# Placing the norm steps of the next batch by when GpSimd has their input, in an attention and feed-forward kernel

## The chip, the cores and the metric

The kernel runs on one core of one Trainium2 chip. The metric is device time in microseconds (us). (The clock is the share of full speed that was granted to PE.)

Names of the engines as the profile has them: PE is TensorE, PEld its weight loads, DVE is VectorE, ACT is ScalarE, POOL is GpSimd, SP is the engine whose queue issues most DMAs. ACT and DVE take their instructions in program order.

## The reference, cut to what matters

```python
batch, n_heads, seq, head_dim = 8, 12, 448, 64
q_n, k_n = rmsnorm(q, g_q), rmsnorm(k, g_k)       # x / sqrt(mean(x*x) + 1e-6) * g
attn = softmax(q_n @ k_n.T / 8)
x = (attn @ v).transpose(0, 2, 1, 3).reshape(3584, 768)
h = x @ w_in                                       # 768 -> 2048
g = h + sin(alpha * h) ** 2 / alpha                # "snake"
out = g @ w_out                                    # 2048 -> 768
```

## The kernel before: the parts that matter

For each batch there is an attention stage (21 scores tiles `S`, each a set of small matmuls and one exp on ACT; 6 `A`, each the product with v and a normalization) and a first product (96 matmuls, with the snake on ACT, POOL and DVE). The second product of the *previous* batch is cut into 56 fillers `F` (two matmuls each) and laid between the S and A of the attention stage, so that PE has work while ACT does the exps. The numbers in `S_(3)` are warm-ups: matmuls on a blank tile, whose results nobody uses. Matmuls write to PSUM, a memory in banks; DVE copies (`osb`) take the second product out of it, and PE waits when no bank is free.

q and k come in three chunks per batch (`NC = 3`). Each chunk is normalized in steps, on three engines (1/sqrt is made of a Ln and an Exp):

```python
st.steps = (lambda: square(0), lambda: square(1), # 0, 1: POOL, q and k
            fold_g,                               # 2: POOL, q *= g_q*g_k
            lambda: reduce(0), lambda: reduce(1), # 3, 4: DVE, sums of the squares
            lambda: (rsqrt(), scale(0), scale(1)),# 5: ACT Ln and Exp, then POOL
            transpose)                            # 6: SP, DMA transposes
```

During the attention stage of batch b, the last steps of its own third chunk (c2) and nearly all steps of the next batch's first two (c3 and c4) are handed out over 24 slots of the plan:

```python
PLAN = "6 SS 7 SS 7 SSS 8 SSS 8 SSAS 7 SS 5 SSASA 4 S 4 SSAAA"   # numbers: fillers
at[s0].append(step_of(ci, 5))                 # c2, s0 = 2
at[s0 + 2].append(step_of(ci, 6))
if b + 1 < B:
    for ci in (NC * b + 3, NC * b + 4):       # c3 from slot 2, c4 from slot 10
        at[s0] += [lambda ci=ci: begin_norm(ci), step_of(ci, 0, 1, 2)]
        for n, step in ((4, 3), (5, 4), (6, 5), (8, 6)):
            at[s0 + n].append(step_of(ci, step))
        s0 += 8
```

`begin_norm(ci)` also loads chunk ci+2 into one of three buffers. A stage's place on the clock is written "+x" below: x us after the stage began.

## Time and profile before

| | before |
|---|---|
| time, median | 467.0 us |
| first product of batch 0 starts | 47.2 us |
| from there to the first product of batch 1 | 58.0 us |
| from one first product to the next, batches 1 to 6 | 53.44 us each |
| the same, batch 6 to 7 (no next batch to norm) | 50.35 us |
| from the last first product to the end | 43.4 us |

The starts of the eight first products are read from the chain of work that ended last; they mark the batches, because each is 18.28 us of matmuls without a stop. Sum of the stretches: 47.2 + 58.0 + 5 x 53.44 + 50.35 + 43.4 = 466.1, the profiled span. The lines themselves are in the prediction. Two more, from the list of who waited for whom over the whole span (us in total, times, longest):

```profile
ACT inv L235 <- DVE ms L226: 28.2, 13, 3.2
DVE ms L226 <- POOL sq L220: 21.6, 11, 5.6
```

ACT stood 28 us at the Ln of a norm and DVE 22 us at a reduce, each for want of its input.

### The profile page before, as it was taken

To read this page: it belongs to the slowest core of one execution; us is meant where nothing else is said; L and a number is where in the kernel's file an instruction comes from. 1 tells how busy PE (TensorE), PEld (TensorE's weight loads), DVE (VectorE), ACT (ScalarE), POOL (GpSimd) and SP (SyncE) were. 2 spreads that over 40 slices of the span, in tenths; PEclk is the share of its full clock that TensorE was granted. 3 is DMA by queue.
4 is the path that set the end of the run, shared out by engine and by line. 5 is a ranking of instruction groups with operands and counts; after the bars stand their busy time and mean duration, and the time that the engine had idled before them with its cause. 6 is when DMAs were issued, how large, how long until landed. Compare 5 with 4: busy or idle time off the path is not lost.

```text
span 466.1 us, 9452 instructions
## 1 busy us (share of the span) xinstructions
PE 431.0 (92%) x3810; PEld 224.4 (48%) x3812; DVE 227.7 (49%) x331; ACT 340.3 (73%) x531; POOL 278.1 (60%) x262
## 2 busy tenths in 40 slices
PE   7777996899998999989998999989998999999996
PEld 3235543455544555445544555445544555555563
DVE  3575572335734564445643546254644456144521
ACT  4768784587867788688877878767877878788800
POOL 3858869554699086963789266981879455201400
PEclk9788997999999999999999999999999999999999
DMA  6999997684065900787046920679026720410023
GB/s 237 192 242 241 232 170 211 148 108 114 0 147 161 203 28 2 189 178 168 1 111 184 166 76 1 163 178 195 3 77 151 89 63 1 108 36 18 1 50 86
DMA packets 69296, 55.09 MB, mean 118 GB/s; under 512 B 41460, under 2 KB 65796, under 8 KB 69252
## 3 DMA queue, kind: packets, MB, share of 16 engines
q1 hardware_dynamic: 56690, 40.97, 35.5%
q0 software_dynamic: 11616, 11.81, 17.8%
q10 hardware_dynamic: 946, 1.70, 1.0%
q8 instruction: 30, 0.49, 0.4%
q14 instruction: 14, 0.11, 0.1%
HBM read 45.62 MB, written 11.01 MB: 122 GB/s over the span
## 4 chain that ended last, share of the span: by engine, by line
PE 62%; ACT 11%; POOL 10%; DVE 9%; issue 5%; DMA 2%; SPq 0%; POOLq 0%; DVEq 0%
PE hps L343 31%; PE ops L388 14%; PE av L307 12%; ACT expT L294 7%; DVE ms L226 5%; POOL qkn L245 4%; POOL sq L220 4%; PE sc L291 4%; DVE xT L316 1%; ACT inv L235 1%; POOL s L325 1%; DVE g_sb L330 1%; PE sc L287 1%; DMA qkT<-qkn 1%; ACT inv L236 1%
## 5 line engine op out<-in xcount | busy, mean ns | idle before, releaser
L294 ACT ACTIVATE expT<-sc 128x896 bf16<-128x896 f32 x168 | 144.1, 912 | 30.8 <-PE sc L291 30.6
L388 PE MATMUL ops<-w_out_sb,g_sb 128*128 128x384 bf16 x896 | 159.9, 330 | 5.3 <-ACT expT L294 5.3
L343 PE MATMUL hps<-xT,w_in_sb 128*128 128x448 bf16 x768 | 146.7, 353 | 0.0
L325 POOL TENSOR_TENSOR s<-s 128x448 f32<-128x448 f32 x64 | 59.3, 930 | 120.0 <-ACT s L322 109.1
L388 PEld LDWEIGHTS <-g_sb 128*128 128x128 bf16 x896 | 83.5, 98 | 77.9 <-issue 27.4
L330 DVE SCALAR_TENSOR_TENSOR g_sb<-s,inv_alpha_sb,hps 128x448 bf16<-128x448 f32 x128 | 80.7, 677 | 63.1 <-POOL s L325 63.1
L343 PEld LDWEIGHTS <-w_in_sb 128*128 128x128 bf16 x768 | 74.3, 98 | 71.7 <-issue 2.9
L316 DVE TENSOR_TENSOR xT<-av,rec 64x448 bf16<-64x448 f32 x96 | 59.7, 622 | 88.8 <-ACT rec L311 69.7
L322 ACT ACTIVATE s<-hps,alpha_sb 128x448 f32<-128x448 f32 x128 | 74.5, 627 | 28.6 <-PE hps L343 26.7
L245 POOL TENSOR_TENSOR qkn<-qk,inv 128x448 bf16<-128x448 f32 x84 | 76.1, 937 | 28.1 <-ACT inv L236 21.3
L220 POOL TENSOR_TENSOR sq<-qk 128x896 f32<-128x896 f32 x42 | 69.9, 1678 | 7.4 <-DVE ms L226 5.6
L307 PE MATMUL av<-expT,vb 64*64 64x448 bf16 x672 | 70.7, 356 | 3.6 <-ACT expT L294 3.6
L307 PE MATMUL av<-expT,ones 64*64 64x448 bf16 x672 | 70.9, 356 | 0.0
L291 PE MATMUL sc<-qkT 64*64 64x448 bf16 x672 | 53.8, 374 | 15.0 <-ACT expT L294 7.5
L226 DVE TENSOR_REDUCE ms<-sq 128x14 f32<-128x896 f32 x42 | 44.9, 1082 | 21.9 <-POOL sq L220 21.6
L223 POOL TENSOR_TENSOR qk<-qk,gg 128x896 f32<-128x896 f32 x24 | 50.0, 2084 | 5.0 <-ACT gg L171 3.4
L394 DVE COPY osb<-ops 128x768 f32<-128x768 f32 (+1 forms) x35 | 27.9, 798 | 47.1 <-PE ops L388 46.3
L307 PEld LDWEIGHTS <-vb 64*64 64x64 bf16 x672 | 39.5, 109 | 15.9 <-issue 5.4
L307 PEld LDWEIGHTS <-ones 64*64 64x64 bf16 x672 | 38.6, 109 | 10.6
L327 ACT ACTIVATE s<-s 128x448 f32<-128x448 f32 x64 | 36.9, 577 | 2.8
L291 PEld LDWEIGHTS <-qkT 64*64 64x64 bf16 x672 | 16.4, 107 | 45.1 <-issue 40.4
L310 ACT ACTIVATE rec<-av 128x448 f32<-128x448 f32 x48 | 26.2, 545 | 4.1 <-PE av L307 3.6
(43 smaller groups left out, 137.6 us busy)
## 6 DMA issues: line engine op xcount, KB each, us to landing
qk<-in_q_dram SPq DMA_DIRECT2D x24, 448.0 KB, 6.1
qk<-in_k_dram SPq DMA_DIRECT2D x22, 448.0 KB, 6.9
out_dram<-osb SPq DMA_DIRECT2D x39, 192.0 KB, 4.6
vb<-in_v_dram POOLq DMA_DIRECT2D x32, 168.0 KB, 7.4
w_in_sb<-in_moe_w_in_dram POOLq DMA_DIRECT2D x2, 1536.0 KB, 19.3
w_out_sb<-in_moe_w_out_dram POOLq DMA_DIRECT2D x2, 1536.0 KB, 25.8
out_dram<-osb SPq DMA_DIRECT2D x26, 96.0 KB, 3.1
qk<-in_k_dram ACTq DMA_DIRECT2D x2, 448.0 KB, 5.8
```

The costliest lines, as they stand in the source:

```text
L220: nc.gpsimd.tensor_mul(st.sq[w], qk[ci][:, w], qk[ci][:, w])
L226: nc.vector.reduce_sum(st.ms[:, w, :], st.sq[w], axis=AX.X)
L245: eng.tensor_mul(n[:, :, hi, :], x[:, hi], inv[:, hi].unsqueeze(2).to_broadcast([P, NJ, D]))
L291: nc.tensor.matmul(sc[key_rows(pp, hi), pp, :S], qkt[r, 1, j * REST:(j + 1) * REST], qkt[r, 0, :], start=True, stop=True)
L294: nc.scalar.activation(expT[c, j], sc[:, :, :S], ACT.Exp, scale=SCALE)
L307: nc.tensor.matmul(av[o, part, :S], ones[r, :] if part else vb[b][r, hp, j, :], expT[pi // 2, j][r, pi % 2, :], start=(j == 0), stop=(j == ...
L316: nc.vector.tensor_mul(xT[b][r, hp, :], av[r, 0, :S], rec[o, :])
L322: nc.scalar.activation(s1, hps, ACT.Sin, scale=alpha_sb[:, m, :])
L325: nc.gpsimd.tensor_mul(s2, s1, s1)
L330: nc.vector.scalar_tensor_tensor(g_sb[:, m, (b % 2) * S:(b % 2 + 1) * S], s2, inv_alpha_sb[:, m, :], hps, op0=ALU.mult, op1=ALU.add)
L343: nc.tensor.matmul(ps[:, m % 2, :S], w_in_sb[:, kt, m * P:(m + 1) * P], x[:, kt, :], start=(kt == 0), stop=(kt == KT - 1))
L388: nc.tensor.matmul(st["ps"][:, k, :HALF], lhsT, w_out_sb[:, m, half * HALF:(half + 1) * HALF], start=(m == 0), stop=(m == MT - 1))
```

## The change

Its intent: give each norm step a slot by which its input exists, so that no in-order engine waits with ready work behind it. To fill POOL's wait for c3's Ln, the squares of c4 go ahead of c3's scale. The chunk loads move behind the transposes of the chunk that frees the buffer, and the loads of v go out two slots later. The order of batch 0, which has no second product to fill with, is redone by hand.

```diff
-                    lambda: (rsqrt(), scale(0), scale(1)), transpose)
+                    lambda: (rsqrt(), scale(0), scale(1)),
+                    lambda: (transpose(), load_qk(ci + 3) if ci + 3 < NC * B else None))
...
     def begin_norm(ci):
         norm[ci] = norm_tasks(ci)
-        if ci + 2 < NC * B and ci != NC + 2:
-            load_qk(ci + 2)
... (batch 0: S, A and warm-up matmuls in another order; its core:)
-    S_(), S_(3), S_(4)
+    S_(2), S_(1), S_()
     c1.pe_transpose((0, 1))
+    load_qk(NC + 1)
     c2.reduce(0), c2.reduce(1)
-    S_(), S_(3), A_(), S_()
+    S_(), S_(1), S_(1)
     c2.rsqrt()
     c2.scale(0), c2.scale(1)
...
-    S_(3), S_()
+    A_(), S_(1), S_(1), S_(1)
     c2.pe_transpose((0, 1))
... (batches 1 to 7:)
-        at[s0].append(step_of(ci, 5))
-        at[s0 + 2].append(step_of(ci, 6))
+        at[2].append(step_of(c2, 5))
+        at[7].append(step_of(c2, 6))
...
+            at[2] += [lambda: begin_norm(c3), step_of(c3, 0, 1, 2)]
+            at[10] += [lambda: begin_norm(c4), step_of(c4, 0, 1)]
+            for slot, task in ((9, step_of(c3, 3)), (10, step_of(c3, 4)), (12, step_of(c3, 5)), (12, step_of(c4, 2)),
+                               (13, step_of(c4, 3)), (15, step_of(c4, 4)), (17, step_of(c3, 6)), (18, step_of(c4, 5)),
+                               (23, step_of(c4, 6))):
+                at[slot].append(task)
```

More of the change, by code (lines that the diff above doesn't have):

```diff
@@ L469 @@
     load_qk(NC)
-    S_(), S_(3), S_(4)
+    S_(2), S_(1), S_()
     c1.pe_transpose((0, 1))
+    load_qk(NC + 1)
     c2.reduce(0), c2.reduce(1)
-    S_(), S_(3), A_(), S_()
+    S_(), S_(1), S_(1)
     c2.rsqrt()
     c2.scale(0), c2.scale(1)
-    load_qk(NC + 1)
+    load_qk(NC + 2)
     load_w_out(0)
@@ L485 @@
     step_of(NC + 1, 0, 1, 2)()
-    S_(), S_(), S_(), S_(), S_()
+    S_(), S_(), S_()
     step_of(NC, 3, 4)()
-    A_(), S_()
+    A_(), S_(1), A_(), S_(1)
     step_of(NC, 5, 6)()
-    A_(), S_()
+    S_(1), A_(), S_(1)
     step_of(NC + 1, 3, 4)()
+    S_()
     v_parts[2](), v_parts[3]()
     load_w_out(1)
-    S_(), S_(), A_()
-    step_of(NC + 1, 5)()
     A_(), A_()
-    step_of(NC + 1, 6)()
+    step_of(NC + 1, 5, 6)()
     first_product(0, beside_h(0))
@@ L509 @@
         n_fill = len(fillers) - (KEPT if b % 2 == 0 else 0)
-        at = [[] for _ in range(SLOTS + 8)]
-        s0, ci = 2, NC * b + 2
-        if b == 1:
-            load_qk(ci + 2)
-        at[s0].append(step_of(ci, 5))
-        at[s0 + 2].append(step_of(ci, 6))
-        if b + 1 < B:
-            for ci in (NC * b + 3, NC * b + 4):
-                at[s0] += [lambda ci=ci: begin_norm(ci), step_of(ci, 0, 1, 2)]
-                for n, step in ((4, 3), (5, 4), (6, 5), (8, 6)):
-                    at[s0 + n].append(step_of(ci, step))
-                s0 += 8
+        at = [[] for _ in range(SLOTS)]
+        c2, c3, c4 = (NC * b + 2 + n for n in range(3))
+        at[2].append(step_of(c2, 5))
+        at[7].append(step_of(c2, 6))
+        if b + 1 < B:
+            at[2] += [lambda: begin_norm(c3), step_of(c3, 0, 1, 2)]
[4 more added lines that the diff above has]
+                at[slot].append(task)
             for n, part in enumerate(load_v(b + 1)):
-                at[s0 - 1 + n].append(part)
+                at[19 + n].append(part)
         S_, A_ = stage(b)
```

## The prediction

> **What bounds the kernel now.** I read the page first: who is busy, and in which slices.
>
> ```profile
> span 466.1 us, 9452 instructions
> PE 431.0 (92%) x3810; PEld 224.4 (48%) x3812; DVE 227.7 (49%) x331; ACT 340.3 (73%) x531; POOL 278.1 (60%) x262
> PEclk9788997999999999999999999999999999999999
> ```
>
> TensorE (PE) idles 35 us in all, and its granted clock dips at the start and once more in slice 6 (70 to 82 us). Next I cut the span into stages by the blocks of `hps` matmuls that the chain of work that ended last passes through (18.3 us each), and asked for busy time in each stretch. Columns: stretch and length, busy (instructions) of PE, weight loads, DVE, ACT and POOL, then clock, DMA share, GB/s.
>
> ```profile
> 0.00:47.20 47.20, 35.96 (x383) 17.17 (x386) 25.69 (x43) 33.21 (x53) 30.76 (x37) 0.86 0.97 228
> 65.50:105.15 39.65, 32.83 (x349) 16.76 (x348) 15.94 (x24) 27.40 (x41) 24.97 (x24) 0.91 0.80 155
> 177.00:212.00 35.00, 32.47 (x365) 17.09 (x363) 16.20 (x21) 27.30 (x41) 24.89 (x23) 1.00 0.61 131
> 212.00:230.40 18.40, 18.40 (x102) 9.53 (x99) 10.93 (x17) 14.38 (x25) 11.65 (x10) 1.00 0.34 91
> 390.60:422.67 32.07, 32.07 (x365) 16.81 (x364) 11.98 (x18) 26.56 (x37) 4.67 (x6) 1.00 0.24 59
> ```
>
> The first products are pure PE. All the idle lies in the attention stages: batch 0, batch 1 (39.65), and five like the third row (35.0 to 35.1). The last row is the yardstick: batch 7 does the same 365 matmuls without any norm work for a following batch, and PE never stops: 32.07. So the norm steps cost a steady stage 3.0 us, though neither DVE nor POOL is full. The timeline of batch 2 says how (start, length, instruction, idle before it and its releaser):
>
> ```profile
> 131.78 3.32 POOL L220 TENSOR_TENSOR sq<-qk 128x896 f32<-128x896 f32 x2
> 135.13 1.08 DVE L226 TENSOR_REDUCE ms<-sq 128x14 f32<-128x896 f32 x1 [0.55 <-POOL sq L220]
> 136.25 0.32 ACT L235 ACTIVATE inv<-ms,eps 128x28 f32<-128x28 f32 x1 [2.21 <-DVE ms L226]
> 137.68 1.46 PE L388 MATMUL ops<-w_out_sb,g_sb 128*128 128x384 bf16 x8 [1.05 <-ACT expT L294]
> 145.72 0.32 ACT L235 ACTIVATE inv<-ms,eps 128x28 f32<-128x28 f32 x1 [2.63 <-DVE ms L226]
> 147.15 0.38 PE L291 MATMUL sc<-qkT 64*64 64x448 bf16 x4 [1.06 <-ACT expT L294]
> 147.95 0.38 PE L307 MATMUL av<-expT,vb 64*64 64x448 bf16 x2 [0.42 <-ACT expT L294]
> ```
>
> ACT, in order, stands at the Ln of a norm whose squares GpSimd has only just made; the exps behind it are late, and PE runs out of PSUM banks or of `expT`: 1.05 + 1.06 + 0.42 = 2.53 us. Batch 1 has the same fault on DVE:
>
> ```profile
> 75.51 1.09 DVE L226 TENSOR_REDUCE ms<-sq 128x14 f32<-128x896 f32 x1 [5.57 <-POOL sq L220]
> 77.12 0.59 PE L291 MATMUL sc<-qkT 64*64 64x448 bf16 x4 [3.99 <-DVE osb L394]
> ```
>
> The reduce waits 5.57 us for squares, the output copy (`osb`) behind it is late, and PE waits 3.99 us for that bank; a second such wait takes 2.11 us at 91.4.
>
> **What the Trainium skill says.** "Perfetto Trace Analysis", Optimization Strategy: find the gaps of the engine you optimize and what blocks it there; done above. The same page, Sequencer Loop: an engine instruction is queued and waits there for its semaphores; the rows above agree and show that later ready work of that engine waits too. "TensorE: Matmul & The Clock Gate", What's actually happening: after an idle window of about 3.4 us the clock is halved. This trace agrees roughly: batch 1, with its 3.99 us gap, has a mean clock of 0.91, stages with gaps of 1 us have 1.00. "GPSIMD Engine Reference", Elementwise: about 2.6 cycles per element for two inputs, an estimate of 1.9 us for 896 at 1.2 GHz; here 2.08 (fold of g) and 1.68 (square). I use the trace's.
>
> **The change part by part.** Nothing of substance is added or removed: one warm-up matmul fewer, the same norm instructions and bytes. It moves three things.
>
> *Norm steps, batches 1 to 6.* GpSimd's order was: scale c2, squares c3, fold c3, scale c3, squares c4, fold c4, scale c4. Now squares c4 come before scale c3. The reduces of c3 go from slots 6 and 7 of 24 to 9 and 10, its Ln from 8 to 12; c4's reduces go to 13 and 15, its Ln from 16 to 18. I lay GpSimd out from its start (+4.95 us into the stage: 128.20 against 123.25) with the trace's durations: scale c2 3.6 to +8.6; squares c3 3.3 to +11.9; fold 2.1 to +13.9; squares c4 to +17.2; scale c3 to +20.8; fold c4 to +22.9; scale c4 to +26.4. Last reduce of c3 is then done at +11.9 + 1.1 = +13.0, and of c4 at +18.3. When do the in-order engines arrive? I take batch 7's unstalled times: slot 12 falls behind the tenth exp, which ACT ends at +14.0 (and later with the Ln/Exp of c2); slot 18 at about +20.7. Both come after their input. DVE meets the first reduce of c4 about 1 us early (+14.4 against +15.6), but the next work behind it is due at +17.6. All three PE waits should go, and the stage comes down from 35.05 to about 32.35 (yardstick plus 0.3 for the Ln/Exp pairs): 2.7 x 5 = 13.5 us.
>
> *Batch 1.* It has 16 matmuls fewer than batch 7 (x349 against x365), so unstalled 32.07 - 16 x 0.166 = 29.4 (0.166 from 2.77 us for 16 back to back). Its half-width output units need a copy every 16 matmuls, so DVE blocking bites harder here: the first reduce (slot 9, about +8.9) still waits for squares at +10.2 with a copy due at +9.7 behind it. I allow 3 us of stalls: 32.5, a gain of 7.1. With no 4 us gap the clock stays up.
>
> *Batch 0.* ACT sets the pace. Its idle from 14.4 us to the end is about 6 us. Fewer warm-ups ahead of the c1 transposes, and c2's Ln and scale ahead of the first attend, save some 1.7 and then 2 to 3 us, about 4 by the c2 transposes. But I do not count all of it, because of these rows:
>
> ```profile
> 38.13 1.68 POOL L220 TENSOR_TENSOR sq<-qk 128x896 f32<-128x896 f32 x1 [1.79 <-DMA qk<-in_k_dram]
> 47.86 3.62 POOL L245 TENSOR_TENSOR qkn<-qk,inv 128x448 bf16<-128x448 f32 x4
> 51.48 1.16 ACT L322 ACTIVATE s<-hps,alpha_sb 128x448 f32<-128x448 f32 x2 [1.78 <-PE hps L343]
> ```
>
> Squares of c4 wait for k to land at 38.1 with the DMA share at 0.97, and what follows on GpSimd is the same and full until 51.4. The first snake square stands behind it. If PE reaches the first product at 43.5 rather than 47.2, that square still ends at 52.4, DVE frees the first bank pair at 53.6, and PE stops at its fifth pair. From there four pairs at 2.28 us: end at 62.7, not 65.5. Gain 2.8.
>
> *Loads behind transposes.* In steady stages transposes land in 3.2 to 6.0 us and nobody waits for them: gain 0. It matters only at 47 us, where four transposes hold the SP queue for 17.3 us and land 13 to 16 us after issue.
>
> Sum: 2.8 + 7.1 + 13.5 = 23.4 us. The products and the 25 us tail stay.
>
> **The rivals.** (a) The wait moves: c3's scale is now 3.3 us later on GpSimd, so its transposes and c4's come later, and the next stage may wait for `qkT`. For: c4's scale still ends at +26.4 with 4 to 6 us to landing. Against: that is within the stage, and c4 is first read 9 us into the next attention stage. If it bit, 2 us per stage would come back: 455. (b) GpSimd is the bound and PE only waits elsewhere, for instance at the first product. Against: 24.9 busy of 35.0, and after its last scale GpSimd idles 11 us. It would leave about 460. (c) DMA in the first 70 us is the bound: batch 1 comes sooner, but c4's transposes, behind the load of chunk 6 in the same queue, land at about 70 to 75 as before while PE wants them at 62.7 + 9.5 = 72. That would cost up to 3 us: 447. (d) The batch 0 gain passes in full, and batch 1 needs only 30.5: 440.
>
> **Range and chances.** 467.3 - 23.4 is 443.9; I shade for (c) and (a) to 445. The range 439 to 452 runs from (d) to a steady gain of 1.7 and a batch 1 gain of 5. 2% is 458.0: that needs less than half of the sum, so faster 0.93, within 0.06, slower 0.01.
>
> **What would show it.** Right: the third row's stretch near 32.3 with no Ln row that waits over 1 us for `ms`; batch 1 near 32.5 at clock 1.00; no 4 us PE gap for `osb`; first product of batch 0 ending near 62.7 with PE stopped for GpSimd or DVE. Wrong: PE rows released by a transpose or a load, GpSimd busy with c4's scale when the first product starts in steady stages, or the same sum of PE idle under another releaser.

## The result, and the profile after

The changed kernel takes 442.19 us (four runs, 442.11 to 442.57) against 466.99 us before. The ratio is 0.948, 95% interval 0.945 to 0.952.

The head of the page after: the same instructions, PE 97% busy instead of 92%, and one dip of the clock, between 11 and 33 us, where the kernel before had several.

```profile
span 440.3 us, 9454 instructions
PE 425.9 (97%) x3811; PEld 220.4 (50%) x3811; DVE 228.1 (52%) x331; ACT 340.1 (77%) x531; POOL 278.0 (63%) x262
PEclk9679999999999999999999999999999999999999
```

The stretches that answer to those of the prediction (length, then busy time and instructions of PE, PEld, DVE, ACT, POOL, then clock, DMA share, GB/s): batch 0, and the attention stages of batches 1, 2 and 7.

```profile
0.00:44.48 44.48, 36.41 (x384) 15.89 (x385) 25.56 (x42) 32.65 (x51) 29.07 (x35) 0.85 0.95 229
62.76:94.84 32.08, 30.07 (x349) 15.74 (x348) 15.95 (x24) 27.42 (x41) 24.99 (x24) 1.00 0.95 196
113.12:145.19 32.07, 32.07 (x365) 16.81 (x364) 16.31 (x22) 27.42 (x41) 24.99 (x24) 1.00 0.54 140
364.87:396.96 32.09, 32.09 (x366) 16.82 (x364) 11.97 (x18) 26.56 (x37) 4.68 (x6) 1.00 0.25 59
```

A stage that norms two chunks of the next batch (third row) now takes what a stage without them takes (fourth row), and PE is busy for every 0.01 us of it. DVE, ACT and POOL do what they did before. Of what batch 1 gained, 2.8 us is PE's own busy time: the same 349 matmuls took 32.83 us before, at a mean clock of 0.91, and take 30.07 us at 1.00. Where the 25.8 us of span came from, by the starts of the first products:

| stretch | before | after | gain |
|---|---|---|---|
| start to first product of batch 0 | 47.18 | 44.48 | 2.70 |
| to that of batch 1 | 57.97 | 50.36 | 7.61 |
| to those of batches 2 to 6 | 5 x 53.44 | 5 x 50.35 | 15.40 |
| to that of batch 7 | 50.35 | 50.35 | 0 |
| to the end | 43.43 | 43.34 | 0.09 |

The timeline of batch 2 after (start, length, instruction, idle before it and its releaser; the stage began at 113.12):

```profile
123.18 1.09 DVE L226 TENSOR_REDUCE ms<-sq 128x14 f32<-128x896 f32 x1 [2.66 <-POOL sq L220]
124.82 1.09 DVE L226 TENSOR_REDUCE ms<-sq 128x14 f32<-128x896 f32 x1 [0.55 <-POOL sq L220]
126.36 0.96 DVE L395 COPY osb<-ops 128x768 f32<-128x768 f32 x1 [0.45 <-PE ops L389]
126.99 0.33 ACT L235 ACTIVATE inv<-ms,eps 128x28 f32<-128x28 f32 x1
134.02 0.32 ACT L235 ACTIVATE inv<-ms,eps 128x28 f32<-128x28 f32 x1
```

Both Ln rows have no idle time in front: their input was there. The DVE reduces of c3 still wait 2.66 and 0.55 us for squares, the same as in batch 2 before. Their old and their new slots lie between the same two output copies, so in a steady stage this move leaves DVE's order as it was, and the gain there cannot come from it. The wait is free: the copy behind it then waits for PE in turn (0.45 us), so DVE was back before there was anything else to do. The list of waits says the same for the whole span:

```profile
DVE ms L226 <- POOL sq L220: 27.2, 17, 2.7
ACT inv L235 <- DVE ms L226: 0.8, 2, 0.5
```

ACT's waits at Ln fell from 28.2 to 0.8 us. DVE's waits at reduces *rose* from 21.6 to 27.2 us, in a kernel that is 25 us faster: the length of a wait does not say what it costs. What is left of PE's waits in batch 1:

```profile
74.42 2.11 PE L389 MATMUL ops<-w_out_sb,g_sb 128*128 128x384 bf16 x12 [0.71 <-DVE osb L395]
81.60 0.57 PE L292 MATMUL sc<-qkT 64*64 64x448 bf16 x8 [0.99 <-DVE osb L395]
```

And in batch 0, the rows on POOL that the prediction leaned on:

```profile
37.08 1.68 POOL L220 TENSOR_TENSOR sq<-qk 128x896 f32<-128x896 f32 x1 [1.44 <-DMA qk<-in_k_dram]
50.41 1.81 POOL L326 TENSOR_TENSOR s<-s 128x448 f32<-128x448 f32 x2
```

### The profile page after: what moved, and what is told of

It reads as the page before. It is cut to its first block, busy times and chain, and to the rows that moved or that the text cites. A ratio compares the mean times of both kernels' runs of the same rounds, so it can differ in the third digit from the quotient of the medians.

```text
span 440.3 us, 9454 instructions
## 1 busy us (share of the span) xinstructions
PE 425.9 (97%) x3811; PEld 220.4 (50%) x3811; DVE 228.1 (52%) x331; ACT 340.1 (77%) x531; POOL 278.0 (63%) x262
## 4 chain that ended last, share of the span: by engine, by line
PE 85%; ACT 4%; POOL 3%; issue 2%; DVE 2%; DMA 2%; SPq 0%; POOLq 0%; DVEq 0%
PE hps L344 33%; PE ops L389 32%; PE av L308 12%; PE sc L292 8%; ACT expT L295 3%; POOL sq L220 2%; DMA g_rows<-in_g_q_dram 1%; POOL qk L223 1%; DMA out_dram<-osb 1%; DVE qkn L245 1%; POOL qkn L245 1%; DVE ms L226 0%; ACT rec L311 0%; PE tp L267 0%; DVE g_sb L331 0%
## 5 line engine op out<-in xcount | busy, mean ns | idle before, releaser
L389 PE MATMUL ops<-w_out_sb,g_sb 128*128 128x384 bf16 x896 | 156.8, 327 | 0.8 <-DVE osb L395 0.7
L245 POOL TENSOR_TENSOR qkn<-qk,inv 128x448 bf16<-128x448 f32 x84 | 76.1, 937 | 21.8 <-ACT inv L236 21.3
L226 DVE TENSOR_REDUCE ms<-sq 128x14 f32<-128x896 f32 x42 | 45.3, 1083 | 27.5 <-POOL sq L220 27.2
L292 PE MATMUL sc<-qkT 64*64 64x448 bf16 x672 | 52.1, 369 | 2.7 <-DVE qkT L274 1.1
L308 PEld LDWEIGHTS <-vb 64*64 64x64 bf16 x672 | 37.8, 108 | 15.4 <-issue 3.3
L308 PEld LDWEIGHTS <-ones 64*64 64x64 bf16 x672 | 37.3, 108 | 10.8
L292 PEld LDWEIGHTS <-qkT 64*64 64x64 bf16 x672 | 15.1, 106 | 30.6 <-issue 25.8
```

Source lines behind the costliest of these rows:

```text
L245: eng.tensor_mul(n[:, :, hi, :], x[:, hi], inv[:, hi].unsqueeze(2).to_broadcast([P, NJ, D]))
L292: nc.tensor.matmul(sc[key_rows(pp, hi), pp, :S], qkt[r, 1, j * REST:(j + 1) * REST], qkt[r, 0, :], start=True, stop=True)
L308: nc.tensor.matmul(av[o, part, :S], ones[r, :] if part else vb[b][r, hp, j, :], expT[pi // 2, j][r, pi % 2, :], start=(j == 0), stop=(j == ...
L389: nc.tensor.matmul(st["ps"][:, k, :HALF], lhsT, w_out_sb[:, m, half * HALF:(half + 1) * HALF], start=(m == 0), stop=(m == MT - 1))
```

## The experiments

Theory: what costs PE time is an instruction that stands in an in-order queue (Ln on ACT, a reduce on DVE) before its input exists *while work that PE needs is ready behind it*. Rivals: the order on POOL is what matters; the place of the loads matters; the first stage carries the gain. Twelve kernels were run; all gave correct results.

**The three parts of the change, each alone on the kernel before.** The first takes only the `at[...]` lines of the diff (and keeps the loads where they were), the second only the order of batch 0, the third only the loads.

p1_slots (norm steps alone):

```diff
+        at[7].append(step_of(c2, 6))
+            at[2] += [lambda: begin_norm(c3), step_of(c3, 0, 1, 2)]
+            at[10] += [lambda: begin_norm(c4), step_of(c4, 0, 1)]
+            for slot, task in ((9, step_of(c3, 3)), (10, step_of(c3, 4)), (12, step_of(c3, 5)), ...
```

> The kernel before with the new places of the norm steps in batches 1 to 6 alone; loads and first stage as before. Theory (the norm steps at the head of the ACT and DVE queues before their squares exist are what stops PE in steady stages): steady attention stages come down from 35.05 to about 32.1, batch 1 from 39.65 to 32 to 33, the first product of batch 0 still starts at 47.2; the time is about 444 to 446. Rival (the loads issued behind transposes matter, or the first stage carries it): steady stages stay above 34 and the time above 455.

p2_first (batch 0 alone):

```diff
-    S_(), S_(3), S_(4)
+    S_(2), S_(1), S_()
-    S_(), S_(3), A_(), S_()
+    S_(), S_(1), S_(1)
...
```

> The kernel before with the new order of the first stage alone. Theory: the first product of batch 0 starts at about 44.5 instead of 47.2, everything later is as before (batch 1 near 39 to 40, steady stages 35.05); the time is 2 to 3 us less, about 464. Rival (the gain of batch 0 is eaten because batch 1 then waits longer for its chunks): no change in the time.

p3_loads (loads alone):

```diff
-                    ... scale(0), scale(1)), transpose)
+                    ... scale(0), scale(1)), lambda: (transpose(), load_qk(ci + 3) if ...))
-            load_qk(ci + 2)
```

> The kernel before with the chunk loads issued behind the transposes alone (chunk 5's load stays where its norm begins). Theory: nobody waits for transposes or chunk loads in steady stages, so 0 us, within 1 us of before. Rival (transposes that land sooner, or loads that collide less, are worth something): 2 us or more.

And the other way round, g_load_first, the changed kernel with each load ahead of the transposes again:

```diff
-                    lambda: (transpose(), load_qk(ci + 3) if ci + 3 < NC * B else None))
+                    lambda: (load_qk(ci + 3) if ci + 3 < NC * B else None, transpose()))
```

> The changed kernel with each chunk load issued ahead of the same chunk's transposes instead of behind. Theory: within 1 us of the changed kernel, 442, with PE without a wait for transposes. Rival: c4's transposes, which end at about +26 of 32 us in a stage and land behind 0.9 MB of load, come too late for the next stage: 1 us or more per stage, 447 or above.

| run | median | ratio to before | first product of batch 0 | stage of batch 1 | steady stage |
|---|---|---|---|---|---|
| p1_slots | 443.36 | 0.950 (0.948 to 0.953) | 47.34 | 32.08 | 32.09 |
| p2_first | 465.09 | 0.996 (0.994 to 0.998) | 44.51 | 38.69 | 35.16 |
| p3_loads | 467.41 | 1.001 (0.997 to 1.005) | 45.86 | 39.85 | 35.16 |
| g_load_first | 442.15 | 0.947 (0.946 to 0.949) | 44.34 | 32.08 | 32.08 |

The norm slots alone give 0.050 of the change's 0.052; the order of batch 0 gives 0.004; the loads give nothing either way, and no load by itself hurts. With the loads first, the transposes of batch 2 land a median 5.7 us after issue instead of 3.3, and nobody waits for them there. (PE waited for a transpose once, 0.41 us in batch 1, without an effect on the stage.) Two readings of the table need care. In p2_first the stage of batch 1 is 1.0 us shorter than before (38.69 against 39.69) with the same stops of 3.99 and 2.11 us; its mean clock is 0.96 instead of 0.91, so this is not the work of the edit that is tested. And the first product's start varies by about 1 us between executions whose instructions ahead of it are the same (43.79 in f_pool_order, 44.84 in e_ln_early, both below), so whether the 45.86 of p3_loads, which also moves a load of batch 0, is the edit's doing is not shown.

**ACT: Ln early again.** e_ln_early puts the Ln/Exp of c3 and c4 straight behind their reduces; POOL and DVE keep the order of the change.

```diff
-                    lambda: (rsqrt(), scale(0), scale(1)),
+                    lambda: (None if st.inv else rsqrt(), scale(0), scale(1)),
...
+  (10, lambda: norm[c3].rsqrt()), ... (15, lambda: norm[c4].rsqrt()), ...
```

> The changed kernel with the Ln/Exp of c3 and c4 put straight behind their reduces in the program (slots 10 and 15 instead of 12 and 18); GpSimd's and DVE's order unchanged. Theory: ACT stands at c3's Ln for about 2 us again (it arrives at about +10.8, its input is there at +13.0), PE stops for exps for about 1 us or more in each steady stage: stages of 33 to 34.5, time 448 to 456. Rival (GpSimd's order is what counts, and it is unchanged here): 442 to 443.

Measured: 455.05 us, ratio 0.974 (0.973 to 0.976). The steady stage takes 34.17 us; from its timeline and its stretch:

```profile
128.53 0.32 ACT L235 ACTIVATE inv<-ms,eps 128x28 f32<-128x28 f32 x1 [2.22 <-DVE ms L226]
129.96 1.46 PE L389 MATMUL ops<-w_out_sb,g_sb 128*128 128x384 bf16 x8 [1.06 <-ACT expT L295]
115.70:149.87 34.17, 32.62 (x365) 17.20 (x364) 16.31 (x22) 27.43 (x41) 25.00 (x24) 1.00 0.59 142
```

The pair of waits of the kernel before is back with its old sizes (there 2.21 and 1.05), at an ACT row moved by two slots of the plan, with POOL's new order in place. So two of the 3.1 us per steady stage are ACT's position alone, and for c3 POOL's order does not cure it. For c4 it is different: ACT still stands 1.63 us at its Ln (2.63 before), but of the two PE stops behind it only the one of 0.42 us is left, and the one of 1.06 us is gone, though this Ln is no later in the plan (slot 15, before 16). Its input is there at +21.3 instead of +22.3, since c4's squares come sooner on POOL; an earlier input was enough for that stop.

**DVE: reduces early again.** d_reduce_early puts c3's reduces at slots 6 and 7 and c4's at 10 and 11, with the Ln late. d2_reduce_c3 moves only c3's.

```diff
-  (9, step_of(c3, 3)), (10, step_of(c3, 4)), ... (13, step_of(c4, 3)), (15, step_of(c4, 4))
+  (6, step_of(c3, 3)), (7, step_of(c3, 4)), ... (10, step_of(c4, 3)), (11, step_of(c4, 4))   # d_reduce_early
+  (6, step_of(c3, 3)), (7, step_of(c3, 4)), ... (13, step_of(c4, 3)), (15, step_of(c4, 4))   # d2_reduce_c3
```

(In d_reduce_early the squares of c4 also begin two slots earlier in the program, with the same order on POOL.)

> The changed kernel with the reduces of c3 and c4 put back early on DVE (slots 6, 7 and 10, 11 of 24), the Ln/Exp left late. Theory: DVE then stands at a reduce without input with output copies behind it; batch 1 with its half-width output units loses most of what it gained (stage 35 to 37 instead of 32.1), steady stages lose little, 0 to 1 us each; the time is 445 to 450. Rival (only ACT's Ln matters): the time is that of the changed kernel, 442.

> The changed kernel with only c3's two reduces early on DVE (slots 6 and 7 instead of 9 and 10), c4's where the change has them. In the run with both pairs early a steady stage lost 5.8 us, all behind c4's pair. Theory (a wait in a queue costs what stands ready behind it): in steady stages the next output copy is due at about +13.3, after c3's reduces are done at +13, so 0 lost, stages 32.1; in batch 1, with a copy every 16 matmuls, the copy behind is late by 3 us or more and PE waits about 4 us: stage 36 to 38; time 446 to 448. Rival (any reduce placed before its input costs its own wait): steady stages lose 1 us or more too, time above 450.

Measured: d_reduce_early 480.23 us, ratio 1.029, *slower than before*; d2_reduce_c3 448.05 us, ratio 0.960 (0.957 to 0.963). The expectation for the first was a miss: steady stages lost 5.8 to 7.2 us, not 0 to 1. Its batch 2, a reduce of c4 on DVE and the next PE stop, then the stop's own stretch and the one behind it, and at last the whole stages of batches 2 and 3:

```profile
134.38 1.09 DVE L226 TENSOR_REDUCE ms<-sq 128x14 f32<-128x896 f32 x1 [2.60 <-POOL sq L220]
138.02 0.59 PE L292 MATMUL sc<-qkT 64*64 64x448 bf16 x4 [4.22 <-DVE osb L395]
133.80:138.02 4.22, 0.00 (x0) 0.00 (x0) 3.04 (x3) 0.92 (x1) 4.22 (x5) 0.94 0.23 87
138.02:142.00 3.98, 3.98 (x41) 2.30 (x41) 0.00 (x0) 1.70 (x3) 3.58 (x3) 0.64 0.66 152
118.98:156.88 37.90, 33.68 (x365) 17.69 (x364) 16.22 (x22) 27.65 (x41) 25.01 (x24) 0.95 0.56 130
175.15:213.92 38.77, 34.55 (x365) 17.84 (x364) 16.22 (x22) 27.65 (x41) 25.02 (x24) 0.91 0.53 125
```

c4's pair stood in front of the output copy due at about +13.3 and held it until its squares were done, so PE waited 4.22 us for a bank; the clock then fell to a mean of 0.64 for the next 4 us. All five steady stages have this stop of 4.22 us, but the clock took more in some than in others: PE was busy for 33.64 to 35.04 us, against 32.07 in the changed kernel. The clock was at 0.50 for 3.41 us in batch 2 and for 6.83 us, twice that, in batch 3. The stop had ended 0.51 us into the slow stretch in batch 2 (from 137.51) and 2.07 us into it in batch 3 (from 192.12). In all eleven stops of 2.86 us and more, over all runs, it goes with this: 3.41 us where the stop reached at most 0.58 us into the slow stretch, 6.83 where it reached 0.75 us or more. The second run shows that c4's pair is what costs here: with c4's reduces late again, the steady stage is 32.08 us. It tests c3's reduces in batch 1 only. In the steady stage their earlier slots give the same order on DVE as the changed kernel's, and the same waits, 2.66 and 0.55 us. In batch 1, with an output copy every 16 matmuls, each of them gets ahead of one copy, and the two cost 6.3 us (38.36 against 32.08):

```profile
75.34 0.59 PE L292 MATMUL sc<-qkT 64*64 64x448 bf16 x4 [3.99 <-DVE osb L395]
63.67:102.03 38.36, 33.08 (x349) 16.51 (x348) 15.89 (x25) 27.56 (x42) 25.28 (x24) 0.91 0.80 171
```

The stop is that of the kernel before (3.99), and so is the clock (0.91). The rival, that every wait of a reduce costs its own length, falls: 2.66 us cost nothing in the steady stage, and the first wait in batch 1, 5.57 us instead of the changed kernel's 2.62, cost 6.3 us with the clock.

**POOL: the old order.** f_pool_order puts the squares and fold of c4 behind the scale of c3 again, with c4's reduces and Ln late enough to suit.

```diff
-  at[10] += [lambda: begin_norm(c4), step_of(c4, 0, 1)]   ... (12, step_of(c3, 5)), (12, step_of(c4, 2)), (13, ...), (15, ...), (18, ...)
+  (12, step_of(c3, 5)), (12, lambda: begin_norm(c4)), (12, step_of(c4, 0, 1, 2)), (19, ...), (19, ...), (21, step_of(c4, 5))
```

> The changed kernel with GpSimd back in the old order (squares and fold of c4 behind the scale of c3), and c4's reduces and Ln later to suit (slots 19 and 21). Theory: GpSimd idles 1 us or so before the scale of c3 and ends its norm work at about +28 instead of +26.4, which nobody waits for: within 1.5 us of the changed kernel, steady stages 32.1. Rival (the new order on GpSimd is itself needed): steady stages above 33, time above 446.

Measured: 442.16 us, ratio 0.947 (0.945 to 0.948); the steady stage 32.08 us. POOL idled 0.88 us before c3's scale and ended its norm work later; nobody noticed. So the new order on POOL, the change's own description of itself, is not needed once the Ln are late. Late places are: on ACT for c3's Ln, in every stage, and on DVE for c3's reduces, in batch 1.

**POOL in batch 0.** The prediction let POOL set the end of batch 0's first product. i_pool_later adds two spare squares before c4's scale there.

```diff
+    for _ in range(2):
+        nc.gpsimd.tensor_mul(spare, qk[NC + 1][:, 0], qk[NC + 1][:, 0])
     step_of(NC + 1, 5, 6)()
     first_product(0, beside_h(0))
```

> The changed kernel with two spare squares (3.3 us of GpSimd) ahead of the scale of c4 in batch 0, so that GpSimd comes to the first snake square later. Theory (the step of the prediction in which GpSimd sets the end of batch 0's first product): DVE frees the first bank pair at 52.6 + 3.3 = 55.9, PE wants it at 53.6, so the first product ends 2 to 2.5 us later than 62.76, and the time is about 2 us more. Rival (batch 0 has slack there): no change.

Measured: 447.07 us, ratio 0.957 (0.955 to 0.959), so 4.9 us more than the changed kernel and not 2. Its first product, and the stretches of the stop and behind it:

```profile
56.73 10.85 PE L344 MATMUL hps<-xT,w_in_sb 128*128 128x448 bf16 x48 [2.86 <-DVE g_sb L331]
53.87:56.73 2.86, 0.01 (x1) 0.00 (x0) 1.32 (x3) 1.18 (x3) 2.86 (x4) 0.98 1.28 191
56.73:60.50 3.77, 3.77 (x12) 1.55 (x12) 2.81 (x5) 3.28 (x7) 3.50 (x4) 0.56 1.24 230
```

PE does stop, where the prediction said, and 2.86 us is near the 2 to 2.5 expected. The rest is the clock, at 0.56 behind the stop: the 48 matmuls take 10.85 us, against 9.25 for the 48 ahead of it.

**A version that is better?** h_better applies the same rule to batch 0 again (transposes of c1 one tile earlier, c2's Ln one tile earlier, c4's reduces and Ln ahead of the last attends) and moves c3's reduces in batch 1 one slot on. h2_issues_later then also moves POOL's issues of w_out's second half and of two parts of v behind its first snake squares. a_again is the changed kernel beside the first of them.

```diff
-    S_(2), S_(1), S_()
+    S_(2), S_(1)
     c1.pe_transpose((0, 1))
+    S_()
...
-    c2.rsqrt()                       # behind S_(), S_(1), S_(1)
+    c2.rsqrt()                       # behind S_(), S_(1)
...
+    step_of(NC + 1, 5)()             # ahead of v_parts, load_w_out(1) and the last two A_()
...
-            for slot, task in ((9, step_of(c3, 3)), (10, step_of(c3, 4)), ...
+            for slot, task in ((9 + (b == 1), step_of(c3, 3)), (10 + (b == 1), step_of(c3, 4)), ...
# h2_issues_later, besides:
+    side[1] = [lambda: load_w_out(1)] + side[1]
+    side[6] = [v_parts[2], v_parts[3]]
```

> The changed kernel again, on the same chip as the next one, to compare with it: 442 to 442.5, ratio 0.947 to 0.948.

> The changed kernel with the same rule applied once more: in batch 0 the c1 transposes ahead of a scores tile, c2's Ln one tile earlier, c4's reduces and Ln ahead of the last attends, so that GpSimd scales c4 before it issues loads; in batch 1 c3's reduces one slot later. Theory: the first product of batch 0 starts 1 to 2 us before 44.5 and PE does not stop in it; batch 1 loses one of its two waits (0.7 us); time 439.5 to 441. Rival (batch 0 is held by the landing of k for c4 and by GpSimd behind it): first product ends at 62.8 as before, time 441.5 to 442.

> The kernel of the run before (first product from 43.0, but PE stopped 1.54 us in it for GpSimd and ended at 62.8) with GpSimd's issues of the second half of w_out and of two parts of v moved behind its first snake squares (2.5 us of issue that stood between the scale of c4 and the first square). Theory (GpSimd's order behind the late k sets the end of batch 0): first snake square at about 49, PE does not stop, first product ends near 61.3 and the time is about 1.5 us less, 440.5 to 441. Rival (w_out's second half then lands later than batch 1 wants it, near 72, or the squares bunch at the end): batch 1 waits and the time stays at 442 or rises.

Measured: a_again 442.32 us (ratio 0.948, 0.945 to 0.950), h_better 442.43 us (0.949, 0.946 to 0.952), h2_issues_later 441.94 us (0.948, 0.945 to 0.952). None beats the changed kernel beyond noise, so the 439.5 to 441 and 440.5 to 441 that were expected were both missed. In h_better:

```profile
38.23 1.68 POOL L220 TENSOR_TENSOR sq<-qk 128x896 f32<-128x896 f32 x1 [5.09 <-DMA qk<-in_k_dram]
53.86 9.24 PE L344 MATMUL hps<-xT,w_in_sb 128*128 128x448 bf16 x48 [1.54 <-DVE g_sb L331]
```

The first product starts at 43.06, 1.4 us earlier than in the changed kernel, but k for c4 lands at 38.2, POOL comes late to the snake, and PE gives the gain back: 1.54 us. With POOL's issues out of the way (h2_issues_later) the first product runs from 41.91 to 60.2 without a stop. Then PE waits 0.93, 0.47 and 0.26 us at the head of batch 1 for the last snakes, which POOL does late, and later 1.30 us for an output copy: batch 1's product starts at 93.83 instead of 94.84. One us in a profile is about what executions differ by, so no gain is claimed.

## Why the prediction was right, point by point

The forecast was 445 us (439 to 452) with a sum of 23.4 us; measured were 442.19 us and 25.8 us of span.

- **The bound and its cause.** Right. The layout of GpSimd held: its last scale of a steady stage ended at +26.3 (+26.4 foretold). c4's last reduce was done only at +20.0, not +18.3, since DVE took other work first; c4's Ln at +20.9 still found its input, with 0.9 us to spare. The ACT waits went (28.2 to 0.8 us) and came back with their sizes when the Ln alone was put back. The DVE part holds with one sharper word: the steady reduce still waits 2.66 us and costs nothing.
- **Steady stages, "2.7 x 5 = 13.5".** Measured 3.08 x 5 = 15.4. The 0.3 us allowed for two Ln/Exp pairs was not needed: ACT had that much idle time of its own. The other 0.1 us is that the stage before is 35.16 us and not 35.05. This term carries most of the error in the total.
- **Batch 1, "32.5, a gain of 7.1".** Measured 32.08 and 7.61, out of two terms that were each off: the stops were 1.70 us (0.71 and 0.99) instead of 3, and the stage without stops 30.4 us instead of 29.4. PE was busy for 30.07 us there, only 2.0 less than in batch 7, where 2.7 was counted. That the two errors nearly cancel is luck.
- **Batch 0, "gain 2.8 ... end at 62.7".** The end was 62.76, but not in the way told, and that it agrees this closely is luck. PE reached the first product at 44.48, not 43.5, and did not stop in it; k for c4 landed at about 37.1 instead of 38.1, so POOL came to its first snake square at 50.41 and not 51.4. The cap exists all the same: in runs where k landed after 38 us PE did stop there, 0.96 us in f_pool_order and in d2_reduce_c3, and 1.54 us in h_better. The two limits lie within 1 us of each other.
- **Loads behind transposes, "gain 0".** Right, from both sides (1.001 and 0.947).
- **Rivals.** (a), late transposes: one wait of 0.41 us, in g_load_first; none in the changed kernel. (b), POOL as the bound: not in steady stages, where a later POOL cost nothing, but true of batch 0, where 3.3 us more of it cost 4.9. (c), DMA in the first 70 us: no wait for c4's transposes in batch 1; what DMA does set is the arrival of k. (d), 440, was not reached.

Open: why k for c4 lands anywhere from 37.1 to 38.8 us in executions whose instructions ahead of it are the same. No run here isolates it. Nor was it taken apart which of the moves in batch 0 brings the first product forward.

## What to carry to other kernels

For each instruction you place early in an in-order queue, ask when its input exists and what stands ready behind it: a wait of 2.66 us at a reduce was free in one stage, while two reduces that got ahead of output copies cost 6.3 us in another. A stage of the same kernel that lacks the work in question is a good yardstick; here it named the end of the gain (32.07 us) before the change was run. And count a long PE stop as more than itself: the one of 2.86 us cost about 1.6 us more by the lowered clock, those of 4.22 us 1.6 to 3.0 us more.

## What the Trainium skill lacked or had wrong

- "TensorE: Matmul & The Clock Gate", What's actually happening, puts the loss of clock at an idle window of about 3.4 us, in a free-running window. The runs show it with less. In i_pool_later a stop of 2.86 us was enough: 3.77 us at a mean clock of 0.56 followed, and 48 matmuls took 10.85 instead of 9.25 us. In batch 0 of the kernel before no stop in the 3.41 us from 38.35 was longer than 1.44 us, but PE was busy for only 1.20 us of them, and the clock was 0.50 for the next 3.41 us. A single stop of 2.11 us in batch 1 left it at 1.00 (PE busy 1.52 of the 3.41 us from 89.55). So look at PE's busy share over such a stretch, not at the longest stop alone.
- "Perfetto Trace Analysis", Optimization Strategy, lacks that a wait of another engine has no fixed price: waits of DVE at its reduces rose from 21.6 to 27.2 us while the kernel got 25 us faster.
- "DMA: Bandwidth & Descriptors" lacks how long a transpose takes to land beside ordinary DMAs: a median of 3.3 us after issue with the load behind them, 5.7 us with it ahead (batch 2), and 13.3 to 16.3 us in the loaded first 65 us of the kernel before.
